# Gated attention and long convolution: both side banks for every side group, output normalisation on GpSimd, 93 score pairs on VectorE

## Chip, cores and metric
The kernel runs on one core of one Trainium2 chip. The metric is the device time of a launch in microseconds, as the median of several runs.

## The reference
Two branches share the input x (2048 tokens, width 640) and are mixed token by token by a gate.

```python
k_shift = sum over t < 4 of k_pad[:, t:t+S, :] * shift_k[:, 3 - t]
kv = k_shift * v
y = irfft2(rfft2(kv padded to 2S) * rfft2(ssm_k padded to 2S))[:S] + kv * ssm_D
a = q * y                                          # q is x
Q = (x @ wq) in 32 heads of 20;  K = x @ wk;  V = x @ wv      # one K and V for all heads
b = softmax(Q K^T / sqrt(20)) V, heads joined, @ wo
g = sigmoid(sum(x * gate_w))
out = g * a + (1 - g) * b
```

All inputs and the output are bf16. In the kernel the circular convolution of length 2048 is done with cosine and sine tables and matmuls.

## The kernel before
**Attention.** The 2048 query tokens are four blocks of 512, and the 32 heads are eight groups of four. A head group G (0 to 31) is one block and four heads, its keys are 16 tiles j of 128. So there are 32 x 16 x 4 = 2048 score tiles of 128 keys x 512 queries. A score matmul (line 1073, called `qk`) uses 32 rows of the array, so up to three run side by side. The tiles go to ScalarE in units of alternately three and two: `EXP` (line 1105) reads three banks of PSUM (0 to 2) or two (3 and 4) and writes `ETA` or `ETB`. The value matmuls (line 1145, `pv`) add into bank 6 over the 16 tiles of a group; a further column of `vaug` gives the row sums.

**Score pairs on VectorE.** `DVE_J[G]` lists the j of which two of the four tiles do not go to ScalarE. For such a pair `DEXP` issues two score matmuls (`dqk`) into the side banks 5 and 7, copies both with a scale into `dW` (line 1134), and works the exponential out with three passes over 1024 elements (lines 1137, 1138, 1140), the last into `ETd`. Two value matmuls with the negated `vneg` use it. A `dqk` "rides": it is placed beside a running group of scores that leaves its rows free, and if it has waited longer than `PATIENCE` it is placed alone.

**Normalisation.** At the end of a head group `norm` copies bank 6 to `acc` (line 1203), sends the row sums to `den` by DMA, takes the reciprocal (line 1208), writes it to DRAM and reads it back as the broadcast `rbc`, and multiplies `acc` by `rbc` (line 1215). The result goes to DRAM, or in the last block to `oT3`.

**Side work.** The shift convolution (line 1324), the spectra (line 1382), their products on GpSimd (line 1415), the inverse (line 1448), the query projection of the next block (line 992), the output projection of blocks 0 to 2 (`oproj`, line 1477) and a first part of that of block 3 (`part`, line 1239) are groups of matmuls in a side bank, 5 or 7, that end with a copy on VectorE (`evac`). `oproj` and `qproj_next` are given bank 7 alone.

**The order.** A planner (`Scheduler`) runs when the program is built. It walks through time with a cost for each operation (`c_ps`, `c_pool`, `c_mm` and the like), picks the next operation of each engine by priority, and writes a fixed order for each of the five queues; on the chip each engine runs its order and waits on semaphores. For TensorE, scores and value products come first. A side matmul is placed only if it ends by the time at which the next score could start, plus `SLACK`. A side group takes the first free bank of its list; while a `dqk` is waiting to ride, other groups may not take bank 5. Where TensorE would be idle and was busy less than `FILL` of the last 3.4 us, four dummy matmuls are placed (line 1525). The planner treats GpSimd and those VectorE operations that are marked `port` as sharing one port, one at a time.

**Memory.** The region `R2` of SBUF holds one set of tiles after another. Its last set is `wo`, two `oTp` and four `outsb`, the rows of the output on their way to DRAM.

Of the kernel before, what the change touches and what calls it, by code (L numbers as in the profile page):

```python
# [7 lines left out]
ALU = mybir.AluOpType  # L8
AX = mybir.AxisListType

BF16 = dt.bfloat16
# [3 lines left out]
ENGS = ("sp", "act", "pe", "dve", "pool")  # L15
NLANES = 40
LAT = 0.12
SLACK = 0.2
FILL = 0.65
FWIN = 3.4  # L20
FGAP = 0.1

MODE = {"qk": "r", "dqk": "r", "pv": "c", "fillc": "c"}
SWITCH = 0.096
PATIENCE = 3.0
ROOM = 0.3
OLD = 6.0
PVB = 2
# [121 lines left out]
class Scheduler:  # L150
# [128 lines left out]
    def pick_work(self, t):  # L279
        q = self.main_q["pe"]  # L280
        p = self.main_pos["pe"]
        m = q[p] if p < len(q) else None
        gap = 1e9
        self.gap = 0.0
        if self.float_left:
            f = self.float_left.pop(0)
            return f
        if self.rows and not (m is not None and m.cont):
            best = None
            for gr in self.gcand:  # L290
                if gr.rides and gr.ready <= t and gr.mms[0].row not in self.rows:
                    b = next((x for x in gr.banks if not self.bank_claimed[x] and not self.bank_busy[x]
                              and self.bank_ready[x] <= t), None)
                    if b is not None and (best is None or gr.prio < best[0].prio):
                        best = gr, b
            if best is not None:
                gr, b = best
                self.gcand.discard(gr)
                gr.bank = b
                self.bank_busy[b] = True  # L300
                gr.mms[0].deps.update(self.bank_last[b])
                return gr.mms[0]
        if not (m is not None and m.cont):
            for f in self.floats:
                if f.ready <= t and (self.mode == "c" or t - f.ready > OLD or m is None or m.urge):
                    self.floats.remove(f)
                    self.float_left = list(f.tail)
                    return f
        if m is not None:
            if m.cont:  # L310
                if m.nun == 0:
                    self.main_pos["pe"] += 1
                    return m
                return None
            if m.nun == 0:
                r = m.ready
                ok = True
                for b in m.banks or ():
                    if not self.bank_claimed[b]:
                        if self.bank_busy[b]:  # L320
                            ok = False
                        r = max(r, self.bank_ready[b])
                if ok:
                    if r <= t:
                        self.main_pos["pe"] += 1
                        return m
                    gap = r - t
        sw = SWITCH if self.mode != "f" else 0.0
        self.gap = gap if m is not None else 0.0
        if self.open is not None:  # L330
            gr = self.open
            mm = gr.mms[gr.pos]
            if mm.ready <= t and mm.cost + sw <= gap + SLACK and (sw == 0.0 or gap + SLACK - sw >= ROOM):
                return mm
            return None
        if self.mode != "f" and self.main_started and gap + SLACK - sw < ROOM:
            return None
        best = None
        held = any(gr.rides and gr.ready <= t for gr in self.gcand)
        for gr in self.gcand:  # L340
            if gr.rides and t - gr.ready < PATIENCE:
                continue
            if gr.ready <= t and gr.mms[0].cost + sw <= gap + SLACK:
                b = None
                for x in gr.banks:
                    if held and x == 5 and not gr.rides:
                        continue
                    if not self.bank_claimed[x] and not self.bank_busy[x] and self.bank_ready[x] <= t:
                        b = x
                        break  # L350
                if b is None:
                    continue
                k = (gr.prio, gr.mms[0].seq)
                if best is None or k < best[0]:
                    best = (k, gr, b)
        if best is None:
            if (self.filler0 is not None and not self.main_started and self.busy_in(t, 2.4) < 0.55
                    and all(d.placed and d.end + LAT <= t for d in self.fill0_deps)):
                f = Op("pe", self.filler0, c_mm(512), "c", "fill", 0.0)
                f.deps.update(self.fill0_deps)  # L360
                return f
            return None
        _, gr, b = best
        if gr.rides:
            gr.mms[0].cost = 0.216
        self.gcand.discard(gr)
        self.open = gr
        gr.bank = b
        self.bank_busy[b] = True
        for o in self.bank_last[b]:  # L370
            gr.mms[0].deps.add(o)
        return gr.mms[0]
# [154 lines left out]
S, D, H, DH = 2048, 640, 32, 20  # L527
# [4 lines left out]
HD = 320  # L532
# [9 lines left out]
UP = 256.0  # L542

SIDE = (7, 5)
DVE_J = [(), (), (4,), (6,), (5,), (4, 9, 11), (3, 8, 13), (3, 8, 13), (3, 8, 13), (3, 9, 13), (3, 8, 13), (3, 8, 13), (2, 7, 12), (2, 6, 12), (3, 8, 14), (1, 6, 11), (3, 8, 13), (1, 8, 13), (1, 8, 12), (1, 6, 11), (1, 5, 9, 13), (3, 8, 13), (1, 4, 8, 14), (1, 6, 11), (3, 8, 12), (4, 7, 12), (2, 6, 10, 14), (2, 6, 10, 14), (1, 6, 11), (2, 6, 10, 12), (2, 9, 12), (3, 8, 13)]
MAC_ALT = ()
SCALE = float(DH) ** -0.5

# [1 line left out]
def c_ps(n):  # L550
    return 0.16 + 1.04e-3 * n
# [14 lines left out]
def c_pool(n):  # L566
    return 0.21 + 1.78e-3 * n


def c_mm(n):  # L570
    return 0.005 + 0.417e-3 * n


class Kernel:
# [59 lines left out]
    def alloc(self):  # L634
# [80 lines left out]
        for i in range(2):  # L715
            spec += [(f"ssm_kT{i}", [128, 2, NF, CW], BF16)]
        last = [("wo", [128, NDC, D], BF16), ("oTp0", [128, NDC, 512], BF16), ("oTp1", [128, NDC, 512], BF16)]
        last += [(f"outsb{i}", [128, D], BF16) for i in range(4)]
        region("R2", keep + early0, keep + early, spec + late, last)
        def over(name, under, off, shape, dtype):  # L720
            T[name] = nc.alloc_sbuf_tensor_at(name, shape, dtype, offset=nc.lookup_mloc(T[under]).addr + off)

        over("oT3", "xT", 0, [128, 8, 512], BF16)
        over("part", "xT", 8192, [128, 4, D], F32)
        over("wog", "wq_pad", 0, [128, 8, D], BF16)
# [473 lines left out]
    def norm(self, I, g):  # L1199
# [12 lines left out]
        self.dma(T["rbc"][:, :], bass.AP(sd.tensor, sd.offset, [[512, 4], [0, 32], [1, 512]]),  # L1212
                 reads=[("scr_d", k)], writes=["rbc"], nbytes=262144, prio=p, name="rcp_bc", lat=4.2)
        out, key = (T["oT3"][:, g, :], ("oT3", g)) if last else (T["oTn"][:, :], "oTn")
        self.dve(lambda e: e.tensor_tensor(out, T["acc"][:, :], T["rbc"][:, :], ALU.mult), ["acc", "rbc"],
                 [key], c_ps(512), prio=p, port=True, name="onorm")
        if not last:
            self.dma(self.scr_o[I][128 * g:128 * g + 128, :], T["oTn"][:, :], reads=["oTn"], writes=[("scr_o", I, g)],
                     nbytes=131072, prio=p, name="o_st")
# [11 lines left out]
    def part(self):  # L1231

        T = self.T
        for ci in range(4):
            for half in range(2):
                n0 = HD * half
                gr = self.group("op1", 900.0 + ci)
                for g in range(6):
                    self.mm(gr, lambda e, bk, g=g, ci=ci, n0=n0: e.matmul(
                        self.bank(bk, HD), T["oT3"][:, g, 128 * ci:128 * ci + 128], T["wog"][:, g, n0:n0 + HD],  # L1240
                        start=(g == 0), stop=(g == 5)), [("oT3", g), "wog"], c_mm(HD))
                i = 4 * (NB - 1) + ci
                self.evac(gr, "dve", lambda e, bk, ci=ci, n0=n0, i=i: e.scalar_tensor_tensor(
                    T["part"][:, ci, n0:n0 + HD], self.bank(bk, HD), T["omgf"][:, i:i + 1], T["kv"][:, i, n0:n0 + HD],
                    ALU.mult, ALU.add), ["omgf", ("A", i)], [("part", ci)], c_ps(HD))
# [216 lines left out]
    def oproj(self, I):  # L1462
        T = self.T
        op = T[f"oTp{I % 2}"]
        so = self.scr_o[I].rearrange("(h d) c -> h d c", d=32)
        pr = 640.0 + 60.0 * I
        for dd in range(4):
            self.dma(op[32 * dd:32 * dd + 32, :, :], so[:, dd:20:4, :], reads=[("scr_o", I, g) for g in range(8)],
                     writes=[("oTp", I % 2)], nbytes=163840, prio=-800, name="ld_oT")
        for ci in range(4):  # L1470
            i = 4 * I + ci
            osb = T[f"outsb{i % 4}"]
            for half in range(2):
                n0 = HD * half
                gr = self.group("op", pr + ci, banks=(7,))
                for kc in range(NDC):
                    self.mm(gr, lambda e, bk, kc=kc, ci=ci, n0=n0: e.matmul(
                        self.bank(bk, HD), op[:, kc, 128 * ci:128 * ci + 128], T["wo"][:, kc, n0:n0 + HD],
# [1 line left out]
                self.evac(gr, "dve", lambda e, bk, osb=osb, n0=n0, i=i: e.scalar_tensor_tensor(  # L1480
                    osb[:, n0:n0 + HD], self.bank(bk, HD), T["omgf"][:, i:i + 1], T["kv"][:, i, n0:n0 + HD],
                    ALU.mult, ALU.add), ["omgf", ("A", i)], [("outsb", i % 4)], c_ps(HD))
            self.dma(self.aps["out"][0][128 * i:128 * i + 128, :], osb[:, :], reads=[("outsb", i % 4)],
                     nbytes=163840, prio=-800, name="st_out")

# [7 lines left out]
    def qproj_next(self, I):  # L1493
        if I < NB:
            for b in range(2):
                self.qproj(I, list(range(4 * b, 4 * b + 4)), 150.0 * (I - 1) + 60 + 60 * b, (7,), 4)

    def build(self):
        self.alloc()
# [85 lines left out]
```

## Time and profile before
| | |
|---|---|
| median of three runs | 886.73 us (885.32 to 887.96) |
| profiled execution | 887.47 us, span 885.6 us |
| PE busy | 851.3 us, 96% |
| ScalarE (ACT) busy | 862.2 us, 97% |
| VectorE (DVE) busy | 685.2 us, 77% |
| GpSimd (POOL) busy | 377.3 us, 43% |
| TensorE clock granted | 0.996 of full speed |

Busy time is the time in which an engine had at least one instruction in work; instructions overlap, so the durations of a group can add up to more. A line of a group reads: line, engine, operation, output and inputs, shape, count, then busy time and mean duration, then the engine's idle time just before these instructions and what ended it.

### The profile page before, as it was taken

The numbers are of one execution on the slowest core, as the hardware profiler recorded it, in microseconds if no ns is written. First come the engines' busy times: TensorE is split into PE (matmuls) and PEld (weight loads), VectorE is DVE, ScalarE is ACT, GpSimd is POOL, SyncE is SP. The second block draws the span as 40 slices with busy tenths as digits, with TensorE's granted clock in tenths as the row PEclk, the third lists the DMA queues.
The fourth block names the chain that finished last, engine by engine and source line by source line (L and its number), as shares of the span: only waits on it lengthen the run. The fifth ranks groups of instructions, "written<-read, shape, count | busy, mean of one in ns | idle before, by whom it ended". The sixth has DMA issues, their size and how long they took to land.

```text
span 885.6 us, 17829 instructions
## 1 busy us (share of the span) xinstructions
PE 851.3 (96%) x7736; PEld 347.1 (39%) x7736; DVE 685.2 (77%) x901; ACT 862.2 (97%) x773; POOL 377.3 (43%) x311
## 2 busy tenths in 40 slices
PE   8899999999999999999999999999999999999997
PEld 4335434434443344443333344344334433432233
DVE  6466774398878788878888777888898978897964
ACT  6899999999999999999999999999999999999995
POOL 3930056843534676433762242878044874000000
PEclk9899999999999999999999999999999999999999
DMA  7910300010000010000020200000000002102111
GB/s 170 255 41 14 68 20 11 10 43 21 19 20 5 17 42 21 20 20 10 12 43 20 57 20 13 9 19 20 20 20 20 14 12 67 47 21 69 40 36 38
DMA packets 55779, 31.96 MB, mean 36 GB/s; under 512 B 38547, under 2 KB 51732, under 8 KB 55700
## 3 DMA queue, kind: packets, MB, share of 16 engines
q1 hardware_dynamic: 53562, 29.79, 12.6%
q8 instruction: 60, 0.98, 0.5%
q10 hardware_dynamic: 2138, 1.04, 0.4%
q14 instruction: 19, 0.16, 0.1%
HBM read 17.85 MB, written 6.02 MB: 27 GB/s over the span
## 4 chain that ended last, share of the span: by engine, by line
ACT 83%; PE 12%; DMA 2%; SPq 1%; DVE 1%; issue 0%; DVEq 0%
ACT ETA L1105 50%; ACT ETB L1105 34%; PE ps L1382 5%; PE ps L1073 3%; PE ps L1145 2%; DMA xT<-in_A_q_dram 1%; SPq L1307 1%; DMA kTr<-in_A_k_dram 1%; PE ps L992 1%; PE ps L1324 0%; SPq L597 0%; PE ps L1263 0%; DVE ETd L1140 0%; PE ps L1014 0%; PE ps L1386 0%; DVE dX L1137 0%
## 5 line engine op out<-in xcount | busy, mean ns | idle before, releaser
L1105 ACT ACTIVATE ETA<-ps 128x1536 bf16<-128x1536 f32 x374 | 594.0, 1588 | 5.5 <-PE ps L1073 5.1
L1105 ACT ACTIVATE ETB<-ps 128x1024 bf16<-128x1024 f32 x374 | 436.5, 1167 | 0.1
L1073 PE MATMUL ps<-qT,kT 32*128 32x512 bf16 x2048 | 297.5, 385 | 22.5 <-ACT ETA L1105 13.0
L1415 POOL TENSOR_TENSOR Pp<-X,K 128x512 f32<-128x512 bf16 x120 | 179.9, 1525 | 326.9 <-DVE K L1403 326.7
L1073 PEld LDWEIGHTS ps<-qT,kT 32*128 32x128 bf16 x2048 | 73.5, 91 | 259.3 <-ACT ETB L1105 121.7
L1134 DVE TENSOR_SCALAR dW<-ps 128x512 f32<-128x512 f32 x178 | 122.3, 687 | 47.2 <-PE ps L1073 45.5
L1145 PE MATMUL ps<-ETA,vaug 128*32 128x512 bf16 x1122 | 152.7, 386 | 0.4 <-ACT ETB L1105 0.4
L1145 PE MATMUL ps<-ETB,vaug 128*32 128x512 bf16 x748 | 148.0, 386 | 0.0
L1140 DVE SCALAR_TENSOR_TENSOR ETd<-dX,dW 128x1024 int16<-128x1024 f32 x89 | 123.7, 1389 | 24.1 <-PE ps L1145 23.7
L1137 DVE SCALAR_TENSOR_TENSOR dX<-dW 128x1024 f32<-128x1024 uint16 x89 | 118.9, 1336 | 0.4
L1138 DVE SCALAR_TENSOR_TENSOR dX<-dX,dW 128x1024 f32<-128x1024 f32 x89 | 116.7, 1311 | 0.4
L1415 POOL TENSOR_TENSOR AB<-Pp 128x256 bf16<-128x256 f32 x80 | 90.7, 1134 | 6.0
L1448 PE MATMUL ps<-AB,Tcos 128*128 128x256 bf16 x320 | 76.6, 274 | 0.0
L1448 PE MATMUL ps<-AB,Tsin 128*128 128x256 bf16 x280 | 68.0, 274 | 0.0
L1525 PE MATMUL ps<-Tcos,zeros 128*32 128x512 bf16 x808 | 67.7, 384 | 0.1
L1415 POOL TENSOR_TENSOR Pp<-Pp 128x512 f32<-128x512 f32 x40 | 64.5, 1613 | 3.1
L1382 PE MATMUL ps<-ssm_kT,Tcos 128*128 128x256 bf16 x320 | 54.7, 276 | 0.3 <-DVE X L1395 0.3
L1382 PE MATMUL ps<-ssm_kT,Tsin 128*128 128x256 bf16 x320 | 50.6, 275 | 0.0
L1382 PE MATMUL ps<-kv,Tcos 128*128 128x256 bf16 x320 | 49.2, 275 | 0.1
L1382 PE MATMUL ps<-kv,Tsin 128*128 128x256 bf16 x320 | 48.6, 274 | 0.0
L992 PE MATMUL ps<-xT,wq_pad 128*128 128x512 bf16 x160 | 46.9, 389 | 0.7 <-DMA xT<-in_A_q_dram 0.6
L1145 PEld LDWEIGHTS ps<-ETA,vaug 128*32 128x32 bf16 x1122 | 29.2, 94 | 36.7 <-issue 35.1
(140 smaller groups left out, 743.7 us busy)
## 6 DMA issues: line engine op xcount, KB each, us to landing
rbc<-scr_d SPq DMA_DIRECT2D x31, 256.0 KB
scr_o<-oTn SPq DMA_DIRECT2D x24, 128.0 KB, 1.7
kv<-in_A_v_dram SPq DMA_DIRECT2D x4, 640.0 KB
out_dram<-outsb SPq DMA_DIRECT2D x14, 160.0 KB, 2.5
xn<-in_A_q_dram SPq DMA_DIRECT2D x3, 640.0 KB
oTp<-scr_o SPq DMA_DIRECT2D x12, 160.0 KB, 2.8
wog<-in_B_wo_dram SPq DMA_DIRECT2D x4, 200.0 KB
wo<-in_B_wo_dram SPq DMA_DIRECT2D x4, 200.0 KB, 3.6
```

The source lines that it names most:

```text
L992: o = self.mm(gr, lambda e, bk, gi=gi, dc=dc: e.matmul(self.bank(bk), T["wq_pad"][:, dc, 128 * gi:128 * gi + 128], T["xT"][:, dc, 512 * I: ...
L1073: return e.matmul(self.bank(bk), T["kT4"][32 * r:32 * r + 32, 128 * j:128 * j + 128], T[f"qT{G // 8 % 2}"][32 * r:32 * r + 32, G % 8, :], ...
L1105: op("act", lambda e: e.activation(et(n)[:, 0:w], self.ps[:, lo:lo + w], ACT.Exp, scale=SCALE), [("ps", base[n % 2] + k) for k in range(le ...
L1134: self.evac(gr, "dve", lambda e, bk, h=h: e.tensor_scalar(W[:, 512 * h:512 * h + 512], self.bank(bk), SCALE * LOG2E * 128.0, 128.0 * (127 ...
L1137: V(lambda e: e.scalar_tensor_tensor(X[:, :], w, DP, w, ALU.add, ALU.mult), [kW], ["dX"], c_ps(1024), **k)
L1138: V(lambda e: e.scalar_tensor_tensor(X[:, :], X[:, :], DQ, w, ALU.add, ALU.mult), [kW], ["dX"], c_ps(1024), **k)
L1140: V(lambda e: e.scalar_tensor_tensor(T["ETd"][:, :].bitcast(dt.int16), X[:, :], DA, W[:, :], ALU.mult, ALU.add), [kW, "dX"], ["ETd"], c_ps ...
L1145: return op("pe", lambda e: e.matmul(self.bank(6)[32 * r:32 * r + 32, :], T[va][:, j, :], src, start=(j == 0), stop=(j == NSC - 1), tile_p ...
L1382: self.mm(gr, lambda e, bk, lhs=lhs, rhs=rhs, comp=comp, n=n: e.matmul(self.bank(bk, 256, 256 * comp), lhs, rhs, start=(n == 0), stop=(n = ...
L1415: f = lambda e: e.tensor_tensor(out, a, b, alu)
L1448: self.mm(gr, lambda e, bk, lhs=lhs, fc=fc, comp=comp, h=h: e.matmul(self.bank(bk, 256, 256 * h), lhs, AB[:, fc, :, comp, :], start=(fc == ...
L1525: sch.filler = [[lambda e, r=r, st=st: e.matmul(self.bank(6)[32 * r:32 * r + 32, :], self.T["zeros"][:, 0:32], self.T["Tcos"][:, 0, 0:512] ...
```

## The change
- `DVE_J` has 93 pairs instead of 89, at other places; the first groups have more, and ten groups have four instead of five such groups before.
- The multiplication by `rbc` in `norm` is issued on GpSimd instead of VectorE, with the planner's cost of GpSimd.
- A side group may take bank 5 even while a `dqk` waits to ride. `oproj` and `qproj_next` may take both side banks.
- In `part` the wait for the finished convolution (`("A", i)`) stands on the matmuls as well as on the copy.
- `outsb3` leaves the region `R2` and lies over the first part of `qT0`; the copies into it wait for the last readers of the two slices of `qT0` below it.
- Planner constants: `SLACK` 0.2 to 0.3, `FILL` 0.65 to 0.7, `PATIENCE` 3.0 to 2.5.

```diff
-SLACK = 0.2
-FILL = 0.65
+SLACK = 0.3
+FILL = 0.7
...
-PATIENCE = 3.0
+PATIENCE = 2.5
...
-                    if held and x == 5 and not gr.rides:
+                    if False:
                         continue
...
-DVE_J = [(), (), (4,), (6,), (5,), (4, 9, 11), (3, 8, 13), (3, 8, 13), (3, 8, 13), (3, 9, 13), (3, 8, 13), (3, 8, 13), (2, 7, 12), (2, 6, 12), (3, 8, 14), (1, 6, 11), (3, 8, 13), (1, 8, 13), (1, 8, 12), (1, 6, 11), (1, 5, 9, 13), (3, 8, 13), (1, 4, 8, 14), (1, 6, 11), (3, 8, 12), (4, 7, 12), (2, 6, 10, 14), (2, 6, 10, 14), (1, 6, 11), (2, 6, 10, 12), (2, 9, 12), (3, 8, 13)]
+DVE_J = [(6,), (), (2, 9, 14), (4, 10), (2, 9), (1, 2, 8, 12), (2, 7, 12), (2, 6, 10, 14), (3, 9), (1, 5, 12), (1, 7, 11), (2, 6, 10, 14), (2, 7, 12), (1, 4, 8, 12), (2, 5, 10), (1, 8), (2, 6, 10, 14), (3, 4, 13), (1, 4, 8, 12), (1, 9), (2, 10, 12), (3, 9), (2, 7, 12), (2, 5, 10, 14), (3, 6, 12), (1, 3, 9, 13), (12,), (3, 8, 13), (1, 6, 11), (3, 11, 12), (1, 5, 9, 13), (1, 5, 8, 12)]
...
-        last += [(f"outsb{i}", [128, D], BF16) for i in range(4)]
+        last += [(f"outsb{i}", [128, D], BF16) for i in range(3)]
...
+        over("outsb3", "qT0", 0, [128, D], BF16)
...
-        self.dve(lambda e: e.tensor_tensor(out, T["acc"][:, :], T["rbc"][:, :], ALU.mult), ["acc", "rbc"],
-                 [key], c_ps(512), prio=p, port=True, name="onorm")
+        self.pool(lambda e: e.tensor_tensor(out, T["acc"][:, :], T["rbc"][:, :], ALU.mult), ["acc", "rbc"],
+                  [key], c_pool(512), prio=p, port=True, name="onorm")
...
-                        start=(g == 0), stop=(g == 5)), [("oT3", g), "wog"], c_mm(HD))
+                        start=(g == 0), stop=(g == 5)), [("oT3", g), "wog", ("A", i)], c_mm(HD))
...
+        free = [x for gi in range(2) for x in self.g.readers.get(("qT", 0, gi), ())]
...
-                gr = self.group("op", pr + ci, banks=(7,))
+                gr = self.group("op", pr + ci)
...
+                if i % 4 == 3:
+                    gr.evacs[-1].deps.update(free)
...
-                self.qproj(I, list(range(4 * b, 4 * b + 4)), 150.0 * (I - 1) + 60 + 60 * b, (7,), 4)
+                self.qproj(I, list(range(4 * b, 4 * b + 4)), 150.0 * (I - 1) + 60 + 60 * b, (7, 5), 4)
```

More of the change, by code (lines that the diff above doesn't have):

```diff
@@ L1237, in part @@
                 gr = self.group("op1", 900.0 + ci)
+                i = 4 * (NB - 1) + ci
                 for g in range(6):
@@ L1240, in part @@
                         self.bank(bk, HD), T["oT3"][:, g, 128 * ci:128 * ci + 128], T["wog"][:, g, n0:n0 + HD],
-                        start=(g == 0), stop=(g == 5)), [("oT3", g), "wog"], c_mm(HD))
-                i = 4 * (NB - 1) + ci
+                        start=(g == 0), stop=(g == 5)), [("oT3", g), "wog", ("A", i)], c_mm(HD))
                 self.evac(gr, "dve", lambda e, bk, ci=ci, n0=n0, i=i: e.scalar_tensor_tensor(
```

## The prediction
> **What bounds the kernel now.** I read the page's chain first, then the groups by line, then ScalarE's waits, then the stretches. The chain says which engine sets the end:
>
> ```profile
> ACT 83%; PE 12%; DMA 2%; SPq 1%; DVE 1%; issue 0%; DVEq 0%
> ```
>
> ScalarE carries 83% of the span, all of it the exponentials of line 1105. The groups, shapes kept apart, give the rows that the sums below use (busy time, mean ns, idle time before and its cause):
>
> ```profile
> L1105 ACT ACTIVATE ETA<-ps 128x1536 bf16<-128x1536 f32 x374 | 594.0, 1588 | 5.5 <-PE ps L1073 5.1
> L1105 ACT ACTIVATE ETB<-ps 128x1024 bf16<-128x1024 f32 x374 | 436.5, 1167 | 0.1
> L1140 DVE SCALAR_TENSOR_TENSOR ETd<-dX,dW 128x1024 int16<-128x1024 f32 x89 | 123.7, 1389 | 24.1 <-PE ps L1145 23.7
> L1134 DVE TENSOR_SCALAR dW<-ps 128x512 f32<-128x512 f32 x178 | 122.3, 687 | 47.2 <-PE ps L1073 45.5
> L1137 DVE SCALAR_TENSOR_TENSOR dX<-dW 128x1024 f32<-128x1024 uint16 x89 | 118.9, 1336 | 0.4
> L1138 DVE SCALAR_TENSOR_TENSOR dX<-dX,dW 128x1024 f32<-128x1024 f32 x89 | 116.7, 1311 | 0.4
> L1215 DVE TENSOR_TENSOR oTn<-acc,rbc 128x512 bf16<-128x512 f32 x24 | 21.2, 882 | 2.0 <-DMA rbc<-scr_d 2.0
> ```
>
> The two exponentials add up to more than the span because the end of each record overlaps the start of the next. From start to start in the timeline an undisturbed 1536-wide one takes 1.34 us and a 1024-wide one 0.92 us: 2.26 us for five tiles, 0.452 us a tile. The first starts at 23.24, the last at 874.97. Between them 374 x 1.34 + 373 x 0.92 = 844.3 us are work, so 7.4 us are lost. Adding the excess of every interval over its 1.34 or 0.92 puts 4.8 us of that between 25 and 50 us and 2.6 us in all the rest. From 600 us on nothing measurable is lost. The start's loss is visible on ScalarE and on TensorE:
>
> ```profile
> 37.11 1.45 ACT L1105 ACTIVATE ETA<-ps 128x1536 bf16<-128x1536 f32 x1 [2.46 <-PE ps L1073]
> 41.21 1.45 ACT L1105 ACTIVATE ETA<-ps 128x1536 bf16<-128x1536 f32 x1 [1.49 <-PE ps L1073]
> ```
> ```profile
> 35.54 0.93 PE L1324 MATMUL ps<-kdiag,kTr 128*128 128x128 bf16 x7 [2.10 <-DMA kTr<-in_A_k_dram]
> ```
>
> A shift-convolution group was put in TensorE's order before its transposed load had landed, the scores behind it waited, and TensorE ran slower for some microseconds afterwards (its matmuls of 0.39 us become 0.54 to 0.6). The stretches show who has room:
>
> ```profile
> 30.00:60.00 30.00, 27.67 (x242) 10.81 (x239) 12.59 (x20) 25.59 (x24) 22.03 (x37) 0.89 0.59 149
> 100.00:200.00 100.00, 99.26 (x838) 42.00 (x836) 63.68 (x99) 99.49 (x89) 56.45 (x48) 1.00 0.10 26
> 200.00:300.00 100.00, 97.20 (x849) 39.50 (x848) 82.55 (x102) 99.41 (x89) 47.12 (x30) 1.00 0.06 18
> 800.00:860.00 60.00, 57.34 (x538) 18.24 (x536) 50.06 (x66) 60.00 (x54) 0.00 (x0) 1.00 0.14 44
> ```
>
> Columns are length, then busy time of PE, PE weight load, DVE, ACT and POOL, then clock and DMA. ScalarE is full in every stretch. VectorE has a third free up to 200 us and about 17% later. GpSimd is half idle and wholly idle at the end. TensorE looks full, but 808 of its matmuls (67.7 us, line 1525) are dummies.
>
> **What the Trainium skill says.** "SBUF — State Buffer", Who interferes with whom: a VectorE instruction with two SBUF inputs contends with a GpSimd instruction that reads SBUF, one with at most one SBUF input does not. The trace agrees: of 89 ETd passes the 54 beside an idle GpSimd take 1.22 us, the 28 fully beside a busy one 1.74; the dW copies from PSUM take 0.69 either way. "GPSIMD Engine Reference", Performance versus the Vector engine: a two-input operation there costs about 2.6 cycles an element at 1.2 GHz, so 512 elements are 1.1 us plus dispatch by estimate. The trace has 1.27 us for the f32 add Pp<-Pp where VectorE was idle, 1.79 where it was busy, 1.61 as a mean. "TensorE: Matmul & The Clock Gate", Part 1, says that an idle array is throttled and activity releases it; the clock of 0.89 in the stretch from 30 to 60 agrees.
>
> **The change, part by part.**
> *Pairs 89 to 93.* Four pairs are eight tiles: ScalarE goes from 1870 tiles to 1862, from 748 exponentials to 745 (372 full pairs and one short one). Saved: 8 x 0.452 = 3.6 us, directly on the bounding engine. VectorE pays 2 x 0.687 + 1.336 + 1.311 + 1.389 = 5.4 us a pair, 21.6 us in all. TensorE does the same scores and value products as before. Counted by head group, the pairs move forward: the first six groups have 12 (6 before), groups 20 to 26 have 20 (24 before), the last five 17 as before, but the last two have four each instead of three. The early stretch has the room (63.7% busy from 100 to 200). At the end, 825 to 875, VectorE is busy 34.8 us of 50; two pairs more are 10.8, so 44.2 of 50 after two normalisations leave. It fits, not loosely.
>
> *Normalisation to GpSimd, 31 times.* VectorE loses 24 x 0.882 + 7 x 0.767 = 26.6 us. GpSimd gains 31 x 1.6 = 50 us (bounds 1.27 and 1.8), 377 to 427 us, no bound. While each runs, a two-input VectorE pass beside it is slower by some 0.5 us: 31 x 0.5 = 15 us back at most. Net for VectorE: -26.6 + 21.6 + (0 to 15) = -5 to +10 us of 685. On GpSimd's queue the operation waits for the broadcast rbc. On VectorE it now starts 11.4 to 15.9 us after the copy acc, and in only 3 of 31 cases did it wait for the DMA, 1.2 us at most. Behind it stand the spectral products (line 1415), which themselves wait 327 us for VectorE in total; a microsecond more is hidden by that. Behind the result on SP stand the store of oTn and, from the next group, den and rcp; the next acc comes some 26 us after the last, 10 us later than needed. I take 0, bounds -0.5 and +1.
>
> *Both banks for every side group; dqk no longer keeps bank 5; PATIENCE 2.5.* Output projection and the next block's query projection may alternate banks instead of waiting for one copy after another. This empties the side work sooner (the last part copy ends at 875.2, 1 us ahead of the last value product now). On the other side a dqk matmul more often finds both banks full. Bounds: -1, all side lateness in the middle removed, to +5 (see the rival). I take 0.
>
> *SLACK 0.3, FILL 0.7.* Planned side matmuls may hold a score up 0.1 us longer. After 60 us, 68 of 353 1536-wide exponentials had scores that started 0.2 us or more after the banks came free, and they lost 5.9 us against gains of 2.5 in the others. Only where ScalarE has no stored work does that count, about a third of them up to 400 us, by the records at the shortest duration. 0.05 us on some 50 steps is 2.5 us; bounds 0 and +5. I take +0.4, because most steps there do not reach the limit. More dummies fill only gaps: 0.
>
> *Projection matmuls wait for A instead of their copy; outsb3 over qT0.* A is final near 782 us and the part groups start at 849; the queries that lie under outsb3 are last read before 515, when group 17 ends. Both 0.
>
> Sum on its own span: 885.6 - 3.6 + 0.4 = 882.4. That execution took 887.47; the three runs shown have the median 886.73 (885.32 to 887.96). 886.73 - 3.2 = 883.5 us.
>
> **The rivals.**
> *The start moves too.* A pair now lies in group 0, so dqk matmuls and their copies enter the order at 25 to 35 us, ahead of the group that waited for its load. If the wait shrinks, up to 4.8 us more are saved: about 880. For it: DVE is 42% busy there. Against: the load lands at the same time and the planner knows no more about it.
>
> *Slower: head-of-line blocking by a late VectorE.* One place shows it now:
>
> ```profile
> 231.46 2.01 DVE L1137 SCALAR_TENSOR_TENSOR dX<-dW 128x1024 f32<-128x1024 uint16 x1
> ```
> ```profile
> 234.13 0.38 PE L1073 MATMUL ps<-qT,kT 32*128 32x512 bf16 x1 [0.31 <-DVE dW L1134]
> ```
>
> Two passes were stretched to 2.0 us by GpSimd, the copy of dW came late, the dqk matmul stood at the head of TensorE's order, and ScalarE lost 0.5 us. With both banks shared and 31 more GpSimd reads, this can become common. At 0.5 us each it eats the gain at 7 events; 0.3% slower takes (3.6 + 2.7) / 0.5 = 13 net new ones. At 16 to 20 it gives 891 to 893. For it: ten head groups now have four pairs, five before. Against: groups 26 and 27, four pairs each, ran from 723 to 773 without any loss.
>
> *The gain is eaten.* SLACK at its upper bound and a few such events: 884.1 to 889, no measurable change.
>
> **How the numbers follow.** A measurement of this kernel can tell about 0.3% from no change, 2.7 us: faster is below 884.1, slower above 889.4. The likeliest case, eight tiles less and the losses as they are, 0.52: 882 to 885, of which 0.45 count as faster and 0.07 as the same. Start saved as well, 0.13: faster. Gain eaten, 0.13: the same. Blocking, 0.22: slower. So 0.58, 0.20, 0.22. The range leaves out half of the blocking case and the far half of the start case: 879.5 to 890.5.
>
> **What would show it.** Right: 745 exponentials at 2.26 us a pair, excess of the intervals near 8 us, line 1216 on POOL near 1.6 us each, VectorE near 685 us busy, last value product about 3 us earlier. Wrong: ScalarE's waits for the scores well above 5.1 us, TensorE's score matmuls waiting for dW or for a side copy, or value products waiting for ETd at the end of four-pair groups; or the side work ending after the last value product, so that the tail from the last exponential to the end grows beyond 9.4 us.

## The result and the profile after

| | before | changed |
|---|---|---|
| median (lowest to highest), four runs each | 887.35 us (885.32 to 888.31) | 880.68 us (879.25 to 881.76) |
| span of the profiled execution | 885.6 us | 879.8 us |
| VectorE, GpSimd busy | 685.2, 377.3 us | 683.1, 434.3 us |

The ratio is 0.9927, 95% interval 0.9901 to 0.9952: faster by 6.7 us in the medians, where 3.2 us were forecast. The time lies inside the forecast range.

The chain of the changed kernel says the same of ScalarE as before. Lines are one to four higher, since the diff adds lines.

```profile
ACT 84%; PE 12%; DMA 2%; DVE 1%; issue 0%; SPq 0%; DVEq 0%
```

The groups of the changed kernel, shapes kept apart:

```profile
L1106 ACT ACTIVATE ETA<-ps 128x1536 bf16<-128x1536 f32 x372 | 581.4, 1563 | 1.5 <-PE ps L1074 1.1
L1106 ACT ACTIVATE ETB<-ps 128x1024 bf16<-128x1024 f32 x372 | 425.4, 1144 | 0.0
L1138 DVE SCALAR_TENSOR_TENSOR dX<-dW 128x1024 f32<-128x1024 uint16 x93 | 129.8, 1395 | 1.1
L1139 DVE SCALAR_TENSOR_TENSOR dX<-dX,dW 128x1024 f32<-128x1024 f32 x93 | 125.4, 1348 | 0.4
L1216 POOL TENSOR_TENSOR oTn<-acc,rbc 128x512 bf16<-128x512 f32 x24 | 38.1, 1588 | 90.6 <-DMA rbc<-scr_d 90.5
```

Two units of each size are gone (and one short unit of two tiles stands at the end). ScalarE's idle time before the 1536-wide exponentials fell from 5.5 us to 1.5, of which the wait for scores from 5.1 to 1.1. The normalisation costs 1.6 us on GpSimd. The 90.5 us that GpSimd stood before it are idle time of an engine that is busy half of the span. No computing engine waited for its result; the store of `oTn` on SP did, 22 times and 147.5 us in all, about as before (21 times, 157.7 us).

A span is cut into four terms: start of the first exponential, its work from start to start (1.34 and 0.92 us each), the excess of the intervals over that, up to 60 us (called the start loss below) and after, and the tail from the start of the last exponential to the end.

| | first | work | excess to 60 us | excess after | tail | span |
|---|---|---|---|---|---|---|
| before | 23.2 | 844.3 | 4.8 | 2.6 | 10.6 | 885.6 |
| changed | 25.5 | 840.7 | 1.1 | 1.9 | 10.7 | 879.8 |
| difference | +2.2 | -3.6 | -3.7 | -0.8 | 0 | -5.8 |

The first exponential came later in the profiled execution of the changed kernel because a transposed load of x landed later, and matmuls of the query projection waited 3.1 us for it instead of 0.6. In the other kernels below the first exponential is at 23.6 to 28.1 us with waits of 1.0 to 4.7, while nothing in the change touches these loads. The remaining terms differ by 8.1 us, the medians by 6.7. Each kernel has one profiled execution, so whether the start moves as much between executions of one kernel is not shown.

The start is where the forecast missed most. TensorE in the changed kernel at the time of the old wait, 33 to 37 us, and the one wait that is left in the start:

```profile
34.98 0.23 PE L1325 MATMUL ps<-kdiag,kTr 128*128 128x128 bf16 x1
35.26 0.81 PE L993 MATMUL ps<-xT,wq_pad 128*128 128x512 bf16 x3
36.01 0.39 PE L1074 MATMUL ps<-qT,kT 32*128 32x512 bf16 x3
...
49.82 0.39 PE L1074 MATMUL ps<-qT,kT 32*128 32x512 bf16 x1 [1.07 <-DMA qT<-cr]
```

No shift-convolution matmul waits for its load any more, and the score matmuls keep their 0.39 us. The stretches after:

```profile
30.00:60.00 30.00, 28.32 (x278) 10.93 (x278) 21.35 (x29) 29.05 (x27) 26.47 (x36) 1.00 0.67 164
100.00:200.00 100.00, 98.26 (x862) 38.82 (x863) 78.60 (x116) 99.94 (x91) 57.93 (x42) 1.00 0.12 25
200.00:300.00 100.00, 97.92 (x865) 38.37 (x864) 83.28 (x100) 99.85 (x90) 49.49 (x36) 1.00 0.09 23
800.00:860.00 60.00, 58.87 (x533) 20.14 (x532) 49.26 (x63) 60.00 (x54) 4.07 (x3) 1.00 0.16 50
```

From 30 to 60 us the clock is full instead of 0.89, and VectorE has 21.4 us of work instead of 12.6: the early pairs lie there.

### The profile page after: what moved, and what is told of

Its sections match the earlier page's. It is cut to its first block, busy times and chain, and to the rows that moved or that the text cites. A ratio compares the mean times of both kernels' runs of the same rounds, so it can differ in the third digit from the quotient of the medians.

```text
span 879.8 us, 17975 instructions
## 1 busy us (share of the span) xinstructions
PE 852.8 (97%) x7783; PEld 345.5 (39%) x7804; DVE 683.1 (78%) x890; ACT 858.3 (98%) x770; POOL 434.3 (49%) x342
## 4 chain that ended last, share of the span: by engine, by line
ACT 84%; PE 12%; DMA 2%; DVE 1%; issue 0%; SPq 0%; DVEq 0%
ACT ETA L1106 51%; ACT ETB L1106 34%; PE ps L1074 4%; PE ps L1383 3%; PE ps L1146 2%; DMA xT<-in_A_q_dram 1%; PE ps L993 1%; PE ps L1529 1%; DMA qT<-cr 1%; PE ps L1325 0%; PE ps L1264 0%; DVE qT L1004 0%; PE ps L1015 0%; PE ps L1387 0%; DVE outsb L1288 0%; PE ps L1273 0%
## 5 line engine op out<-in xcount | busy, mean ns | idle before, releaser
L1106 ACT ACTIVATE ETA<-ps 128x1536 bf16<-128x1536 f32 (+1 forms) x373 | 582.7, 1562 | 1.5 <-PE ps L1074 1.1
L1106 ACT ACTIVATE ETB<-ps 128x1024 bf16<-128x1024 f32 x372 | 425.4, 1144 | 0.0
L1074 PE MATMUL ps<-qT,kT 32*128 32x512 bf16 x2048 | 302.1, 384 | 13.4 <-ACT ETA L1106 7.2
L1416 POOL TENSOR_TENSOR Pp<-X,K 128x512 f32<-128x512 bf16 x120 | 174.6, 1474 | 211.0 <-DVE K L1404 207.1
L1135 DVE TENSOR_SCALAR dW<-ps 128x512 f32<-128x512 f32 x186 | 127.5, 686 | 80.8 <-PE ps L1074 79.6
L1138 DVE SCALAR_TENSOR_TENSOR dX<-dW 128x1024 f32<-128x1024 uint16 x93 | 129.8, 1395 | 1.1
L1139 DVE SCALAR_TENSOR_TENSOR dX<-dX,dW 128x1024 f32<-128x1024 f32 x93 | 125.4, 1348 | 0.4
L1216 POOL TENSOR_TENSOR oTn<-acc,rbc 128x512 bf16<-128x512 f32 x24 | 38.1, 1588 | 90.6 <-DMA rbc<-scr_d 90.5
L1529 PE MATMUL ps<-Tcos,zeros 128*32 128x512 bf16 x876 | 72.9, 385 | 0.0
L1216 POOL TENSOR_TENSOR oT<-acc,rbc 128x512 bf16<-128x512 f32 x7 | 12.1, 1732 | 94.1 <-DMA rbc<-scr_d 94.1
```

Of the source, the lines that this page charges most:

```text
L1074: return e.matmul(self.bank(bk), T["kT4"][32 * r:32 * r + 32, 128 * j:128 * j + 128], T[f"qT{G // 8 % 2}"][32 * r:32 * r + 32, G % 8, :], ...
L1106: op("act", lambda e: e.activation(et(n)[:, 0:w], self.ps[:, lo:lo + w], ACT.Exp, scale=SCALE), [("ps", base[n % 2] + k) for k in range(le ...
L1135: self.evac(gr, "dve", lambda e, bk, h=h: e.tensor_scalar(W[:, 512 * h:512 * h + 512], self.bank(bk), SCALE * LOG2E * 128.0, 128.0 * (127 ...
L1138: V(lambda e: e.scalar_tensor_tensor(X[:, :], w, DP, w, ALU.add, ALU.mult), [kW], ["dX"], c_ps(1024), **k)
L1139: V(lambda e: e.scalar_tensor_tensor(X[:, :], X[:, :], DQ, w, ALU.add, ALU.mult), [kW], ["dX"], c_ps(1024), **k)
L1216: self.pool(lambda e: e.tensor_tensor(out, T["acc"][:, :], T["rbc"][:, :], ALU.mult), ["acc", "rbc"], [key], c_pool(512), prio=p, port=Tru ...
```

## The experiments

Theory at the outset: ScalarE's tiles and its start loss set the time, and the parts of the change can be added up. Rivals: the banks made the middle faster; VectorE's relief did; the constants did. Each kernel ran beside the kernel before on its chip; ratios are to that. The table gives the terms of all of them.

| kernel | ratio, 95% interval | first | excess to 60 / after | last inverse copy | last side copy behind last exponential | tail |
|---|---|---|---|---|---|---|
| before | 1 | 23.2 | 4.8 / 2.6 | 781.6 | -0.3 | 10.6 |
| changed | 0.9927 (0.9901 to 0.9952) | 25.5 | 1.1 / 1.9 | 808.5 | 0.7 | 10.7 |
| e1_pool | 1.0220 (1.0203 to 1.0237) | 23.6 | 4.8 / 3.8 | 839.4 | 19.1 | 28.6 |
| e2_pairs | 1.0328 (1.0309 to 1.0347) | 25.4 | 4.0 / 4.1 | 868.9 | 33.4 | 42.9 |
| e4_consts | 1.0238 (1.0221 to 1.0255) | 25.9 | 1.8 / 8.2 | 847.3 | 19.1 | 28.6 |
| e5_ktr | 0.9953 (0.9939 to 0.9968) | 23.8 | -0.2 / 2.7 | 777.3 | -0.3 | 10.7 |
| e3_banks | 1.0010 (0.9996 to 1.0023) | 25.6 | 3.7 / 3.5 | 817.6 | 0.8 | 10.7 |
| e9_op7 | 1.0062 (1.0046 to 1.0077) | 24.5 | 1.0 / 2.0 | 792.9 | 13.1 | 22.6 |
| e10_held | 1.0167 (1.0148 to 1.0185) | 28.1 | 1.0 / 1.6 | 875.9 | 23.0 | 32.4 |
| e6_oldpairs | 0.9962 (0.9950 to 0.9974) | 24.0 | 1.8 / 2.2 | 810.9 | 0.3 | 10.7 |
| e7_nopool | 1.0081 (1.0064 to 1.0098) | 24.1 | 1.2 / 6.0 | 834.0 | 10.4 | 19.8 |
| e8_oldconst | 1.0022 (1.0010 to 1.0034) | 24.7 | 3.4 / 3.4 | 828.7 | 7.8 | 17.2 |
| e12_p96 | 0.9901 (0.9883 to 0.9920) | 24.2 | 3.5 / 2.2 | 805.6 | -4.5 | 10.2 |
| e13_p100 | 1.0031 (1.0022 to 1.0040) | 24.6 | 4.8 / 15.8 | 822.0 | 3.5 | 12.9 |

"Last inverse copy" is the start of the last copy of the inverse transform (line 1458 of the kernel before); the next to last column is the start of the last copy of `oproj` or `part` minus the start of the last exponential. In every kernel where it is over 5 us the tail is 9.4 to 9.5 us more than it.

### The parts alone, put into the kernel before

**e1_pool**: only the normalisation on GpSimd.

```diff
-        self.dve(lambda e: e.tensor_tensor(out, T["acc"][:, :], T["rbc"][:, :], ALU.mult), ["acc", "rbc"],
-                 [key], c_ps(512), prio=p, port=True, name="onorm")
+        self.pool(lambda e: e.tensor_tensor(out, T["acc"][:, :], T["rbc"][:, :], ALU.mult), ["acc", "rbc"],
+                  [key], c_pool(512), prio=p, port=True, name="onorm")
```

> Before, with only the output normalisation moved to GpSimd. Theory (ScalarE's tiles and its waits at the start set the time): no change, ratio 0.998 to 1.002, because VectorE was not the bound: VectorE about 660 us busy instead of 685, GpSimd about 427, the start's wait for the transposed load as before (25 scores stand ahead of the matmul that waits), excess of the exponentials' intervals about 7 us. Rival (VectorE's load is what held the middle up): 1 to 3 us faster, from the intervals after 60 us. Other rival (GpSimd contention): 2 us slower or more, with score matmuls waiting for dW.

Measured: 2.2% slower. Neither the theory nor the first rival holds; the second has the size but not its sign, since no score matmul waited for dW. ScalarE's exponentials lost 1 us more than before; 18 us went into the tail. TensorE after the last exponential (start 876.52):

```profile
878.23 0.85 PE L1477 MATMUL ps<-wo,oTp 128*128 128x320 bf16 x5
879.73 0.85 PE L1477 MATMUL ps<-wo,oTp 128*128 128x320 bf16 x5 [0.65 <-DVE outsb L1480]
881.22 0.85 PE L1477 MATMUL ps<-wo,oTp 128*128 128x320 bf16 x5 [0.64 <-DVE outsb L1480]
...
896.22 0.99 PE L1263 MATMUL ps<-wog,oT 128*128 128x320 bf16 x6 [0.65 <-DVE outsb L1480]
```

Twelve groups of the output projection stand behind the attention, each 1.5 us, because each needs bank 7 and waits for the copy of the one before. The convolution had ended at 839 us instead of 782, so the projection began 66 us later. VectorE was busy 678 us, not 660: its passes beside GpSimd became slower (mean 1.42, 1.37 and 1.43 us for ETd and the two dX instead of 1.39, 1.31 and 1.34).

**e2_pairs**: only the list of 93 pairs.

```diff
-DVE_J = [(), (), (4,), (6,), (5,), (4, 9, 11), ...
+DVE_J = [(6,), (), (2, 9, 14), (4, 10), (2, 9), (1, 2, 8, 12), ...
```

> Before, with only the new list of 93 pairs. Theory: 745 exponentials save 3.6 us, and the matmul that reads the third transposed load now has 27 scores ahead of it instead of 25, so its wait shrinks from 2.1 to about 1 us and the start's loss from 4.8 to about 3: together 4 to 6 us faster, ratio 0.993 to 0.996. Rival (93 pairs need the relief of VectorE): VectorE about 708 us busy, late ETd and dW, excess after 60 us above 5 us, ratio 0.997 to 1.005.

Measured: 3.3% slower. The 3.6 us were saved on ScalarE, the start lost 4.0 us, a little less than before; the convolution ended at 869 us and 22 of the 24 projection copies lie behind the last exponential's start. The rival had VectorE's busy time right (710 us), but the excess after 60 us stayed at 4.1: what came late was not ETd but all the side work. That VectorE's load is the reason is not shown.

**e4_consts**: only the planner's constants.

```diff
-SLACK = 0.2
-FILL = 0.65
+SLACK = 0.3
+FILL = 0.7
...
-PATIENCE = 3.0
+PATIENCE = 2.5
```

> Before, with only SLACK 0.3, FILL 0.7 and PATIENCE 2.5. Theory: 30 scores stand ahead of the matmul that reads the third load, so the start's loss falls from 4.8 to 1 to 3 us; scores are held up longer in the middle, which costs 0 to 5 us: between 3 us faster and 3 us slower. If the constants alone are what made the changed kernel fast, 4 us faster or more; if they do harm in the middle, the intervals after 60 us lose 4 us or more instead of 2.6.

Measured: 2.4% slower. The start's loss fell to 1.8 us as expected, though not by a shorter wait for the load: that is gone, and TensorE waits 1.7 us for a copy that frees a bank instead. That copy stood behind a cast on VectorE of 3.82 us, where its like takes 0.16 (see e8_oldconst). The exponentials after 60 us lost 8.2 us, 4.9 of them in one place at 773 us, and the tail is 28.6 us: the convolution ended at 847 us.

**e3_banks**: only the bank rules, with what goes with them (`outsb3` over `qT0`, the waits in `part`).

```diff
-                    if held and x == 5 and not gr.rides:
+                    if False:
...
-                gr = self.group("op", pr + ci, banks=(7,))
+                gr = self.group("op", pr + ci)
...
-                self.qproj(I, list(range(4 * b, 4 * b + 4)), 150.0 * (I - 1) + 60 + 60 * b, (7,), 4)
+                self.qproj(I, list(range(4 * b, 4 * b + 4)), 150.0 * (I - 1) + 60 + 60 * b, (7, 5), 4)
```

> Before with the bank rules of the change (both banks for every side group, no reserve for dqk, the place of outsb3, the waits in part), but the old pairs, constants and VectorE normalisation. Theory: side work ends earlier, nothing is gained on ScalarE, the start's wait is as before (25 scores ahead): ratio 0.997 to 1.003, last projection copy before 860 us instead of 868, tail 10.7 us. Rival (the banks alone make the changed kernel fast): ratio 0.995 or less.

Measured: no change, as expected. The convolution ended 36 us later than before, and the projection still ended in time, its last copy at 865 us. So the banks alone gain nothing, and they absorb a delay of 36 us. The delays that cost 18 to 32 us of tail with bank 7 alone were larger, 58 to 87 us; the closer comparison is e9_op7 below.

**e5_ktr**: the kernel before, only the planner's figures for the transposed loads of A_k raised.

```diff
-                           nbytes=655360, prio=14 + b, lat=1.6, after=self.crow0, name="ld_k")
-            x.iss = 3.3
+                           nbytes=655360, prio=14 + b, lat=2.2, after=self.crow0, name="ld_k")
+            x.iss = 5.0
```

> Before, with the planner told that each transposed load of A_k takes longer (issue 5.0 instead of 3.3, latency 2.2 instead of 1.6), nothing else: the matmul that reads the third load then has 35 scores ahead of it instead of 25. Theory: the wait of 2.1 us and the slow clock after it go, the start's loss falls from 4.8 to about 1 us, the time by 3 to 4 us, ratio 0.9955 to 0.997, with the old pairs, banks and constants. Rival (the start's wait is hidden later, or comes back as another): ratio 0.999 or more.

Measured: 0.47% faster, as the theory had it. The start loses nothing any more; the other terms are those of before to 0.1 us, but for a first exponential 0.6 us later. ScalarE's wait for scores, 5.1 us in six places before, is

```profile
ACT ETA L1105 <- PE ps L1073: 0.8, 3, 0.5
```

This settles what the start's wait costs: with old pairs, banks, constants and normalisation, its removal alone is worth 0.9953, interval 0.9939 to 0.9968, some 4 us.

### One part taken out of the changed kernel

**e9_op7**: the output projection back on bank 7.

```diff
-                gr = self.group("op", pr + ci)
+                gr = self.group("op", pr + ci, banks=(7,))
```

> The changed kernel with only the output projection put back on bank 7 alone. In the changed kernel the convolution's last copy is at 808 us, 27 us later than before, and the 24 projection copies run from 788 to 853. Theory (two banks for the projection are what lets the other parts pay): the projection groups go one by one, 1.5 us each once the exponentials have ended, some 8 to 16 of them fall behind the last exponential, the tail grows from 10.7 to 22 to 35 us and the time by 12 to 25 us, ratio to the kernel before 1.005 to 1.02. Rival (the tail of the single parts came from elsewhere): within 3 us of the changed kernel, ratio 0.990 to 0.996.

Measured: 1.0062, against 0.9927 some 12 us slower than the changed kernel. The exponentials ran as in the changed kernel to 0.1 us (excess 1.0 and 2.0). The convolution ended at 793 us, only 11 us later than before and 16 us earlier than in the changed kernel, and still nine projection copies fell behind the last exponential:

```profile
871.42 0.85 PE L1479 MATMUL ps<-wo,oTp 128*128 128x320 bf16 x5 [0.74 <-DVE outsb L1482]
872.92 0.85 PE L1479 MATMUL ps<-wo,oTp 128*128 128x320 bf16 x5 [0.65 <-DVE outsb L1482]
```

The theory holds, at the low edge of what it had expected.

**e10_held**: bank 5 kept for a waiting dqk again.

```diff
-                    if False:
+                    if held and x == 5 and not gr.rides:
```

> The changed kernel with only the rule back that side groups may not take bank 5 while a dqk waits. Theory: the convolution ends later still than 808 us, since its groups are refused a bank; if later than about 820 us the projection no longer fits and the tail grows by 0 to 10 us; else the time stays within 2 us of 880.7, ratio 0.991 to 0.995. Rival (the rule protects VectorE from waiting for its scores, so its loss costs something): 1 to 3 us faster than the changed kernel.

Measured: 1.0167, 21 us slower than the changed kernel, more than expected. The convolution ended at 876 us. TensorE did not lack time: it ran more dummies. Line 1529 from 100 to 800 us, first in the changed kernel, then in this one (length, TensorE busy and count, clock, DMA):

```profile
100.00:800.00 700.00, 57.48 (x696) 1.00 0.09 25
```
```profile
100.00:800.00 700.00, 85.39 (x1040) 1.00 0.08 21
```

28 us more of dummies are time in which the order had no side matmul to place, and the rule that refuses a bank is the only edit. How the 28 us become a convolution that ends 67 us later was not followed. Once the convolution is done, the projection with both banks runs without a wait between groups, 15 of its groups and one of `part` in 12.2 us:

```profile
876.57 5.35 PE L1479 MATMUL ps<-wo,oTp 128*128 128x320 bf16 x35 [0.30 <-DVE kv L1459]
881.76 0.98 PE L1241 MATMUL ps<-wog,oT 128*128 128x320 bf16 x6
882.57 6.16 PE L1479 MATMUL ps<-wo,oTp 128*128 128x320 bf16 x40
```

**e6_oldpairs**: the list of 89 pairs.

```diff
-DVE_J = [(6,), (), (2, 9, 14), (4, 10), (2, 9), (1, 2, 8, 12), ...
+DVE_J = [(), (), (4,), (6,), (5,), (4, 9, 11), ...
```

> The changed kernel with the old list of 89 pairs. Theory: 3.6 us more exponentials than the changed kernel; 30 scores ahead of the matmul that waits for the third load, so a start loss of 1 to 3 us as with the constants alone (1.8 us there): 3.5 to 6 us slower than the changed kernel, ratio to before 0.996 to 1.0. VectorE about 660 us busy. Rival (the places of the pairs don't matter, their number neither): ratio 0.991 to 0.995.

Measured: 0.9962, 3.1 us slower than the changed kernel by the ratios; the theory's lower bound was 3.5. Work +3.6, start loss 1.8 instead of 1.1, tail the same; VectorE was busy 675 us, not 660. The places of the pairs were not tested apart from their number. What is left of the start's loss is, as in e4_consts, a wait for a copy behind a long cast (3.79 us).

**e7_nopool**: the normalisation back on VectorE.

```diff
-        self.pool(lambda e: e.tensor_tensor(out, T["acc"][:, :], T["rbc"][:, :], ALU.mult), ["acc", "rbc"],
-                  [key], c_pool(512), prio=p, port=True, name="onorm")
+        self.dve(lambda e: e.tensor_tensor(out, T["acc"][:, :], T["rbc"][:, :], ALU.mult), ["acc", "rbc"],
+                 [key], c_ps(512), prio=p, port=True, name="onorm")
```

> The changed kernel with the output normalisation back on VectorE, 93 pairs, both banks, new constants. Theory (the move relieves VectorE, and without it the convolution ends late): VectorE about 705 us busy instead of 683, the convolution's last copy 10 to 40 us later than 808, so that the projection may fall behind the last exponential: 2 to 15 us slower than the changed kernel. Rival (the move is hidden either way, as its cost was put at 0): within 1.5 us of the changed kernel.

Measured: 1.0081, 13.7 us slower than the changed kernel: VectorE 707 us, last inverse copy at 834, tail 19.8 us and 4 us more of excess after 60 us. As the theory had it.

**e8_oldconst**: SLACK 0.2, FILL 0.65, PATIENCE 3.0.

```diff
-SLACK = 0.3
-FILL = 0.7
+SLACK = 0.2
+FILL = 0.65
...
-PATIENCE = 2.5
+PATIENCE = 3.0
```

> The changed kernel with SLACK 0.2, FILL 0.65 and PATIENCE 3.0. Theory: 35 scores ahead of the matmul that waits for the third load, 25 in the kernel before and 42 in the changed one, and 35 were enough to end that wait when only the planner's figure for the load was raised: start loss about 1 us or less, the rest as in the changed kernel, time within 2 us of it. Rival (the constants carry the gain): 3 us slower or more, with losses after 60 us above 4 us.

Measured: 1.0022, 8.4 us slower than the changed kernel: this expectation fell. The rival has the size, but not its sign: the loss after 60 us is 3.4, not above 4. The wait for the third load is gone, as expected, but another took its place at 34 us. VectorE, GpSimd and TensorE of this kernel:

```profile
32.19 3.02 DVE L846 CAST IndG<-acol 128x4 bf16<-128x4 f32 x1
34.73 0.48 DVE L874 MEMSET Tsinv<- 1x512 bf16 x1
35.44 0.48 DVE L875 MEMSET Tsinv<- 1x512 bf16 x1 [0.23 <-DMA kv<-in_A_v_dram]
35.83 0.61 DVE L1329 TENSOR_TENSOR kv<-ps,kv 128x512 bf16<-128x512 f32 x1
```
```profile
34.42 0.76 POOL L861 COPY Tcos<-Tsin 128x256 bf16<-128x256 bf16 x1
```
```profile
36.50 1.07 PE L1325 MATMUL ps<-kdiag,kTr 128*128 128x128 bf16 x16 [2.25 <-DVE kv L1329]
```

The copy that frees the bank (line 1329) stood behind constant operations on VectorE and came late, because one of them, a cast of four columns, took 3.02 us. The same cast, the fourth of its line, took 3.04, 3.82 and 3.79 us in e2_pairs, e4_consts and e6_oldpairs, and 0.16 to 0.17 us in the other ten kernels. In all four it started within a run of 256-element table operations on GpSimd (lines 861 and 863) and ended 0.02 to 0.03 us after the last of them, the copy `Tcos<-Tsin` shown. So the planner's constants act here through the place of a small operation; what they are worth without it is not shown. And the side work ended 7.8 us behind the last exponential, which adds 6.5 us of tail.

### Further along the same way

**e12_p96** and **e13_p100**: the changed kernel with 96 and 100 pairs, at places searched with the kernel's own planner. The new lists begin

```diff
-DVE_J = [(6,), (), (2, 9, 14), (4, 10), (2, 9), (1, 2, 8, 12), ...
+DVE_J = [(6,), (), (2, 9, 14), (2, 9), (5, 11), (1, 2, 8, 12), ...
```
```diff
-DVE_J = [(6,), (), (2, 9, 14), (4, 10), (2, 9), (1, 2, 8, 12), ...
+DVE_J = [(6,), (), (1, 5, 10, 13), (3, 5, 11, 14), (2, 9), (1, 2, 8, 12), ...
```

> The changed kernel with 96 pairs, their places searched with the kernel's own planner. Theory (ScalarE's tiles set the time as long as side work ends in time): six tiles less are 2.7 us, VectorE about 700 us busy: 2 to 3.5 us faster than the changed kernel, ratio to before 0.989 to 0.991, tail 10.7 us. Rival (VectorE or the side work is at its limit with 93): same or slower, with a longer tail or with score matmuls waiting for dW.

> The changed kernel with 100 pairs, places searched for a shorter time in the same way; side copies end later than the last exponential in the order found. Theory (beyond some 96 pairs the side work on VectorE is what ends last): 14 tiles less are 6.3 us on ScalarE, but the tail or the waits for scores grow by more: 3 to 15 us slower than the changed kernel. Rival (ScalarE is still the only bound): 5 to 6.5 us faster than the changed kernel.

With 96 pairs 0.9901 (0.9883 to 0.9920): 2.3 us faster than the changed kernel by the ratios, as the theory had it, though the intervals of the two overlap. Two more units are gone, the side work ends 4.5 us before the last exponential starts, and the start lost 3.5 us again, 2.7 of them in ScalarE's wait at 48 us (TensorE waits 1.98 us there for the load of `qT`, the one for which the changed kernel waits 1.07). With 100 pairs 1.0031, some 9 us slower than the changed kernel and inside the theory's 3 to 15; but it is not the side work's end that costs it (tail 12.9 us). The exponentials lost 20.6 us, of which 14.2 in three waits of 6.0, 4.6 and 3.6 us. VectorE and then TensorE at the first:

```profile
247.09 1.22 DVE L1141 SCALAR_TENSOR_TENSOR ETd<-dX,dW 128x1024 int16<-128x1024 f32 x1
```
```profile
241.77 0.39 PE L1074 MATMUL ps<-qT,kT 32*128 32x512 bf16 x3
242.09 0.39 PE L1383 MATMUL ps<-kv,Tsin 128*128 128x256 bf16 x2
...
248.41 0.27 PE L1449 MATMUL ps<-AB,Tsin 128*128 128x256 bf16 x1
248.61 0.38 PE L1074 MATMUL ps<-qT,kT 32*128 32x512 bf16 x1
248.93 0.39 PE L1146 MATMUL ps<-ETd,vneg 128*32 128x512 bf16 x2
...
249.47 0.60 PE L1074 MATMUL ps<-qT,kT 32*128 32x512 bf16 x5
```

The head group could not be closed before its last ETd, ready at 248.3 and used at 248.9. The order has no score between 242.2 and 248.6, almost only side matmuls, and the scores that ScalarE waits for come at 249.5. VectorE was busy 82% of the whole span, 728.6 us. It was not full at this place: from 241.3 to 248.3 us it worked 5.0 of 7.0 us and twice stood still for a side matmul. What ended late is the chain of passes of one pair in the planned order; that VectorE as a whole is the bound with 100 pairs is not shown.

## Why the prediction was right, and where it was not

- *What bounds the kernel.* Right: of the changed kernel's 879.8 us, 840.7 are tiles at 2.26 us for five and 3.0 are excess. (That the four terms add up to the span is their definition.)
- *Pairs.* Right in the term. The -3.6 us of work follow from the count of units; in time, e6_oldpairs gives 3.1 us between ratios. It was wrong to take the added 21.6 us of VectorE, at these places, as lying in free time: the list alone, in e2_pairs, costs 32 us of tail.
- *Normalisation on GpSimd.* GpSimd's 1.6 us a piece and VectorE's busy time (683, inside -5 to +10 us of 685) were right; GpSimd's own rose by 57 us, not 50. The value 0 with bounds -0.5 and +1 was wrong: alone it costs 2.2%, and taken out of the changed kernel it costs 13.7 us. Both times most of it is tail, so what decides is when the side work ends, which the term did not ask. Its reading of the Trainium skill was too short in one point: "SBUF — State Buffer", Who interferes with whom, excepts VectorE's 2-port modes from the rule that an instruction with at most one SBUF input does not contend with GpSimd. The cast shown under e8_oldconst has one such input and took 3.02 us beside GpSimd; no run shows in which mode it ran.
- *Both banks.* Put at 0, bounds -1 to +5, with the remark that the side work empties sooner. As a part alone it is 0 (e3_banks). In the changed kernel it is what the other parts stand on: the projection's second bank is worth 12 us there (e9_op7), the end of the dqk rule 21 us (e10_held). The prediction saw that the last part copy ended 1 us ahead of the last value product, and did not follow what happens when that margin is used up: with bank 7 alone every projection group behind it adds 1.5 us (e1_pool), with both banks about 0.8 (e10_held).
- *Start.* The failing term. The sum took no change, and so expected an excess near 8 us; -3.7 us were measured at the start, and 3.0 us of excess in all. The rival that named it, given 0.13, is what happened, but not for its reason. It put the gain down to the pair in group 0. The pairs alone (e2_pairs) lose 4.0 us there, the constants with the old pairs (e6_oldpairs) 1.8. Its reason against, that the planner knows no more about the load, is true; yet 42 scores now stand ahead of the matmul that needs the third load instead of 25, so it no longer waits. e5_ktr shows the same gain without the change. With the pairs alone 27 scores stand ahead and TensorE still waits 2.7 us for the load. With the constants alone 30 stand ahead, and a wait of 1.7 us for the copy behind the long cast is in its place. With the whole change there are 42 and neither wait, and the start loss stays at 1.0 to 1.2 when the normalisation or one of the two bank rules is taken out again (e7_nopool, e9_op7, e10_held). So the start's gain comes with the pairs and the constants together; the constants with the old pairs already have 3.0 of the 3.7 us.
- *SLACK.* +0.4 forecast for the middle, where the loss fell by 0.8. More is lost after 60 us with the new constants in e4_consts (8.2 us) and e7_nopool (6.0), both with late side work; with the same constants e9_op7, e10_held and e6_oldpairs lose 1.6 to 2.2.
- *The rival on the slower side,* a late VectorE at the head of TensorE's order, did not happen at 93 pairs. At 100 it did, through ETd at the end of head groups rather than dW.

What is still open: why each part alone ends the convolution 36 to 87 us later. For the dqk rule the dummies point to the refused bank. For GpSimd's share it is not separated, since both putting it in (e1_pool) and taking it out (e7_nopool) makes the convolution late; each edit makes the planner write another order for all five engines. The places of the pairs were not searched anew for any part, so how much of a loss belongs to the part itself, and how much to a list that fits another order, is not shown either.

The forecast had the right direction with a size that was half, mainly from one start term that it had only as a rival. That the sum came so near is partly luck: pairs, normalisation or constants alone lengthen the tail by 18 to 32 us, and only together with the banks, which were put at 0, is it the old 10.7 us.

## What to carry to other kernels

Where the bounding engine is full, find where the work of lowest priority ends and what it costs once it falls behind the bound: a few microseconds of margin there decide more than the engine's saving. Parts of a change to a planned order can't be priced one by one and added; one that looks free may be the condition of the others. A load that lands later than a planner assumes is worth a look of its own: correcting two figures alone gave some 4 us, about two thirds of this change's gain.

## What was not expected of the hardware

The issue of the two transposed loads of x took 9.23 us in the profiled execution of the kernel before and 11.49 in that of the changed one, with the same SP order up to there, and it moves the first exponential by as much. A cast of four columns on VectorE took 3.0 to 3.8 us in four kernels where its like takes 0.16 to 0.17, and each time ended within 0.03 us of the end of a run of GpSimd's table operations within which it had started. So it looks held until the whole run was over, five or six more operations of some 0.8 us, and not by one of them. By what means is not shown.
